# Regrouping q's columns by heads in a linear-attention block: token-major q tiles, a regrouped weight copy and six M passes

## The chip, the cores and the metric

The kernel runs on one core of a Trainium2 chip. The metric is the device time of one execution in microseconds (us). A core has TensorE (PE, with weight loads shown apart as PEld), VectorE (DVE), ScalarE (ACT), GpSimd (POOL) and SyncE (SP, which here only issues DMAs); each works through its own queue in order, and they meet through semaphores.

## The reference

The input x (2048 tokens of 640 features) is layernormed to xn, and three things are added:

```
qkv = xn @ wqkv                      # 32 heads of 20 features
pq, pk = phi(q), phi(k)              # phi(t) = t+1 if t > 0 else exp(t), + 1e-6
kv  = sum over tokens of pk (x) v    # 20 x 20 per head
z   = sum over tokens of pk
o   = (pq @ kv) / (pq . z + 1e-6)
A   = o @ wo
r   = xn @ w_r;  idx = the 8 tokens with the largest r
y   = (silu(xn[idx] @ w_gate) * (xn[idx] @ w_up)) @ w_down * sigmoid(r[idx])
out = x + A + xn + scatter_add(y at idx)
```

Everything is bf16 in memory, 640 = 5 x 128 features (five chunks), 2048 = 16 x 128 tokens (sixteen tiles).

## The kernel before, in words

The order on every engine is written out by hand: the program text is the order of each queue, nothing is rescheduled.

**Front.** The first x tiles and the weights wk and wq are loaded; VectorE takes batch statistics of each tile (two halves of 320, `ln_half`, L163), `ln_aggr` finishes mean and variance, and from tile 4 on GpSimd makes the scalars in four one-column instructions (L171, L176, L178, L179). `ln_norm` (L186) writes xn, and from tile 3 on issues a DMA transpose on SP's queue (L196) that makes xnT; tiles 0 to 2 are transposed on TensorE.

**Tile loop** (L401, t = 2 to 15; a "slot" below is one t). TensorE does k of tile t (`k_mm`, 10 matmuls: 5 chunks, 512 and 129 columns, token-major: tokens on the partitions), then `ga_mm` of tile t-1 (3 matmuls, part of G = xn^T pk), then q of tile t (`q_mm`, L244, 25 matmuls of 128 columns, feature-major: five blocks m of 128 features on the partitions, so that pqT needs no transpose). The weights of block m are the columns m, m+5, m+10 and so on of wq: a read with a step of 5. ScalarE takes exp and relu of each (`phi_act`); VectorE joins them (`phi_vec`, L225) into pk or pqT. VectorE's queue in a slot: statistics of tile t+3 (t+4 from slot 6 on; slot 5, `CATCH`, does two tiles), normalization of tile t+2 (slot 5 does two, later ones t+3), q_phi of t-1, k phi of t, from slot 12 also residual adds of x and xn. GpSimd makes small constants in slots 3 to 6 (`small_consts`). SP issues the later weight loads, one entry a slot (`late_loads`), behind the transposes; the residual is stored to a DRAM copy `xcp` (`keep`).

**Back half.** The column sums z of pk (`z_mm`), the remaining parts of G (`gb1`, then `gb2` into the PSUM pair gbC, five blocks a tile), eight candidates and their indices on VectorE; GpSimd gathers the 8 token columns into xsT (L537). The denominator `pden` is four column groups of 32 heads by 512 tokens; ScalarE makes its reciprocal as exp(-ln) (L580, L581), and it goes through DRAM (`rscr`) to come back as rows `rb` for all 128 partitions. `norm(j)` (L630) multiplies pqT by it, 512 tokens at a time. `gu` is the gate and up product of the 8 tokens, ScalarE's Sigmoid (which needs a table load, L584) and VectorE make hm, and TensorE transposes it (`ph`). `kv_mm` makes the per-head kv from wv and G, `kv_evict` masks it into kvT. `py` is the down product, stored with an accumulating indirect DMA into xcp (L697), and the residual is loaded back from there in six DMAs (L702).

**M** (L722) is kv @ wo, five chunks of 128 rows by 640 columns. With the step of 5 a group of 32 rows in a chunk belongs to 8 heads, that is to two blocks of 80 features; so each chunk takes two accumulating passes (i), each with four column groups (g) side by side on TensorE and 512 and 128 columns. PAD is the shift that puts the two blocks into the same 32 rows.

**Output** (L753): per tile five chunks by 512 and 128 columns into a PSUM pair (B, A, D, C in turn), VectorE adds the residual from PSUM (L751), and the tile is stored.

Of the kernel before, what the change touches and what calls it, by code (L numbers as in the profile page):

```python
# [8 lines left out]
P = 128  # L9
S = 2048  # L10
D = 640
H = 32
# [13 lines left out]
PAD = 16  # L26
# [3 lines left out]
WARM = 10  # L30
LAST = (0, 320, 512, 640)
CATCH = 5
# [12 lines left out]
def kernel(  # L45
# [42 lines left out]
    wq = sb([P, KC, D], BF16, "wq")  # L88
    wv = sb([P, KC, D], BF16, "wv")
# [3 lines left out]
    kvT = sb([EB, PAD + NEB * KC * 2 * PAD], BF16, "kvT")  # L93

    wd = sb([P, FC, D], BF16, "wd")
    xsT = sb([P, KC, 32], BF16, "xsT")
    hT = sb([P, FC, 32], BF16, "hT")
    rscr = dram.tile([NTB * P, TBLK], BF16, name="rscr")
# [32 lines left out]
    headg = sb([P, NTB, H], BF16, "headg")  # L131
    nc.vector.memset(headg[:], 1.0)
    mask80 = sb([EB, KC, 4, 4], BF16, "mask80")
# [20 lines left out]

    head_select(headg[:], [(0, NTB), (-4, H)], 1, 4)
# [87 lines left out]

    def q_mm(t, tag="B"):  # L244
        ps = pair(tag, f"q{t}")
        for m in range(KC):
            for kc in range(KC):
                nc.tensor.matmul(  # L248
                    ps[:, m * P : (m + 1) * P],
                    lhsT=wq[:, kc, m::KC],  # L250
                    rhs=xnT[:, kc, t * P : (t + 1) * P],
                    start=(kc == 0 and m in (0, 4)), stop=(kc == KC - 1),
                    skip_group_check=True,
                )
        return ps
# [47 lines left out]
    def small_consts(t):  # L303
        if t == 3:
# [5 lines left out]
        elif t == 4:  # L310
# [6 lines left out]
        elif t == 5:  # L317
# [23 lines left out]
    def late_loads(t):  # L341
        def part(dst, src, a, b):
# [4 lines left out]
            2: (x_sb, x_v, 8, 12), 5: (x_sb, x_v, 12, 16),  # L347
            6: (wg, kcF, 0, 2), 7: (wg, kcF, 2, 4), 8: (wg, kcF, 4, 5),
            9: (wu, kcU, 0, 2), 10: (wu, kcU, 2, 4), 11: (wu, kcU, 4, 5),
            12: (wv, wv_v, 0, 2), 13: (wv, wv_v, 2, KC), 14: (wo, wo_v, 0, 4), 15: (wo, wo_v, 4, 8),  # L350
            16: (wd, kcD, 0, 6), 17: (wd, kcD, 6, 12),
        }
        if t in plan:
            part(*plan[t])

# [12 lines left out]
    def q_phi(t, er):  # L368
        phi_vec(pqT[:, :, t * P : (t + 1) * P], er, True)
# [31 lines left out]
    for t in range(2, T):  # L401
# [196 lines left out]
    for t in range(2):  # L598
        gb2(t)
# [207 lines left out]
```

## Time and profile before

| what | value |
|---|---|
| median of 3 runs | 111.74 us (111.49 to 111.99) |
| the profiled execution | 111.62 us, span 109.9 us |
| granted TensorE clock | 1.00 |
| DVE, ACT, POOL busy, share of the span | 78%, 50%, 34% |
| instructions | 2999 |
| HBM read, written | 14.94 MB, 5.81 MB |

The span runs from the first to the last instruction of the execution; the difference to its time lies around it. Times within the trace are us from the start of the span. An entry of a timeline gives start, length, engine, line of the kernel, operation, output<-inputs and, in brackets, how long the engine stood idle before it and what ended that. An entry of the chain of waits gives start, length and what ran; there an instruction counts only until the next one takes over. A row of a group gives the count and then the busy us, the mean ns of one, and the idle time before them. Matmul ends are modelled, and busy TensorE time isn't time at its peak.

### The profile page before, as it was taken

What the parts mean: (1) busy time and instruction counts of PE and PEld (TensorE: products, weight loads), DVE (VectorE), ACT (ScalarE), POOL (GpSimd) and SP (SyncE); (2) the same over time, 40 slices, a digit from 0 to 9 for tenths busy, and PEclk for the clock granted to TensorE, in tenths of its full rate; (3) what the DMA queues carried; (4) which work ended last, traced back from release to release, by engine and by line L of the source; (5) the groups of instructions that cost most, each with busy time, mean ns of one, the idle gap of its engine ahead of it and who ended that gap; (6) DMA issues with size and microseconds to landing.
All of it is one profiled execution on the core that took longest, in us unless ns stands there. A gap on an engine that the chain in (4) does not pass through costs nothing.

```text
span 109.9 us, 2999 instructions
## 1 busy us (share of the span) xinstructions
PE 105.5 (96%) x1183; PEld 69.3 (63%) x1183; DVE 86.1 (78%) x205; ACT 55.1 (50%) x102; POOL 37.9 (34%) x83
## 2 busy tenths in 40 slices
PE   6998999999999999999999999999999999999990
PEld 2456866777577766777667744447995555555560
DVE  6889999887999889875999896951348967698680
ACT  4037987778867797777977745068028000000000
POOL 5414195989889955770000000240008100000000
DMA  2998164930569999998859970899541289997333
GB/s 72 335 375 292 33 36 75 283 66 3 118 177 321 220 267 280 316 305 224 290 187 285 292 257 5 232 378 372 175 145 51 15 228 323 340 387 277 128 119 119
DMA packets 25358, 23.09 MB, mean 210 GB/s; under 512 B 10624, under 2 KB 24064, under 8 KB 25344
## 3 DMA queue, kind: packets, MB, share of 16 engines
q1 hardware_dynamic: 22784, 20.43, 66.5%
q10 hardware_dynamic: 2384, 2.43, 6.4%
q8 instruction: 9, 0.15, 0.6%
q0 software_dynamic: 176, 0.04, 0.6%
q14 instruction: 5, 0.04, 0.1%
HBM read 14.94 MB, written 5.81 MB: 189 GB/s over the span
## 4 chain that ended last, share of the span: by engine, by line
PE 76%; DVE 10%; POOL 8%; issue 3%; DVEq 0%; POOLq 0%
PE o L743 14%; PE k L236 13%; PE q L248 13%; PE gbA L489 6%; PE gaC L259 5%; PE warm L271 4%; PE gbC L590 4%; POOL sq L176 3%; DVE st L163 2%; PE gaD L259 2%; DVE pk L225 2%; PE M L728 2%; POOL sc L178 2%; DVE xn L191 2%; PE gu L606 2%
## 5 line engine op out<-in xcount | busy, mean ns | idle before, releaser
L248 PEld LDWEIGHTS <-wq 128*128 128x128 bf16 x400 | 24.2, 117 | 3.4
L236 PE MATMUL k<-wk,xnT 128*128 128x512 bf16 (+1 forms) x160 | 24.8, 301 | 0.3 <-ACT xnT L206 0.3
L248 PE MATMUL q<-xnT,wq 128*128 128x128 bf16 x400 | 24.9, 220 | 0.0
L743 PEld LDWEIGHTS <-pqT 128*128 128x128 bf16 x165 | 12.8, 98 | 9.3
L236 PEld LDWEIGHTS <-xnT 128*128 128x128 bf16 x160 | 12.3, 98 | 8.5 <-ACT xnT L206 0.9
L213 ACT ACTIVATE eq<-q 128x640 bf16<-128x640 f32 x16 | 11.2, 703 | 10.5 <-PE q L248 10.5
L225 DVE SCALAR_TENSOR_TENSOR pk<-ek,rk 128x640 bf16<-128x640 bf16 x16 | 13.2, 824 | 3.6 <-ACT rk L216 3.4
L743 PE MATMUL o<-M,pqT 128*128 128x512 bf16 x110 | 15.8, 300 | 0.0
L176 POOL TENSOR_TENSOR sq<-sq,half 128x1 bf16<-128x1 bf16 x16 | 12.5, 778 | 6.2 <-DVE sc L175 4.0
L163 DVE BATCH_NORM_STATS2 st<-x_sb 128x6 f32<-128x320 bf16 x32 | 14.1, 480 | 0.4 <-DMA x_sb<-in_A_x_dram 0.4
L225 DVE SCALAR_TENSOR_TENSOR pqT<-eq,rq 128x640 bf16<-128x640 bf16 x16 | 13.2, 823 | 0.7 <-ACT rq L216 0.7
L213 ACT ACTIVATE ek<-k 128x640 bf16<-128x640 f32 x16 | 11.3, 705 | 1.6 <-PE k L236 0.4
L751 DVE TENSOR_TENSOR o_t<-o,x_sb 128x640 bf16<-128x640 f32 x11 | 8.8, 820 | 3.3 <-DMA x_sb<-xcp 1.7
L216 ACT ACTIVATE rq<-q 128x640 bf16<-128x640 f32 x16 | 11.2, 700 | 0.0
L216 ACT ACTIVATE rk<-k 128x640 bf16<-128x640 f32 x16 | 11.2, 699 | 0.0
L259 PE MATMUL gaC<-pk,xn 128*128 128x512 bf16 x32 | 9.5, 378 | 0.2 <-DVE pk L225 0.2
L537 POOL COPY xsT<-xnT 128x5 bf16 x8 | 1.9, 312 | 21.7 <-DVE icol L551 21.7
L178 POOL TENSOR_TENSOR sc<-sq,neg 128x1 f32<-128x1 bf16 x12 | 8.6, 716 | 0.9
L191 DVE TENSOR_SCALAR xn<-x_sb,sc 128x640 bf16<-128x640 bf16 (+2 forms) x17 | 6.9, 412 | 1.2 <-POOL sc L179 1.0
L489 PE MATMUL gbA<-pk,xn 128*128 128x512 bf16 x32 | 7.3, 380 | 0.0
L360 DVE TENSOR_TENSOR x_sb<-x_sb,xn 128x640 bf16<-128x640 bf16 x16 | 7.0, 482 | 0.0
L259 PEld LDWEIGHTS <-xn 128*128 128x128 bf16 x48 | 4.0, 97 | 4.1 <-issue 0.4
(152 smaller groups left out, 120.4 us busy)
## 6 DMA issues: line engine op xcount, KB each, us to landing
xcp<-x_sb SPq DMA_DIRECT2D x4, 640.0 KB, 5.2
x_sb<-in_A_x_dram SPq DMA_DIRECT2D x3, 640.0 KB, 4.7
wd<-in_B_w_down_dram SPq DMA_DIRECT2D x2, 960.0 KB, 6.6
x_sb<-xcp SPq DMA_DIRECT2D x3, 640.0 KB, 6.8
wg<-in_B_w_gate_dram SPq DMA_DIRECT2D x2, 768.0 KB, 6.6
wu<-in_B_w_up_dram SPq DMA_DIRECT2D x2, 768.0 KB, 5.3
out_dram<-o_t ACTq DMA_DIRECT2D x8, 160.0 KB, 2.7
out_dram<-o_t SPq DMA_DIRECT2D x7, 160.0 KB, 3.4
```

What stands on the lines that cost most here:

```text
L163: nc.vector.bn_stats(out=stat[t][:, h, :], in_=x_sb[:, t, h * HW : (h + 1) * HW])
L176: nc.gpsimd.tensor_tensor(out=sq[:, 1:2], in0=sq[:, 0:1], in1=half[:], op=ALU.pow)
L178: nc.gpsimd.tensor_tensor(out=sc[:, 1:2], in0=sq[:, 1:2], in1=neg1[:], op=ALU.pow)
L191: nc.vector.tensor_scalar(out=xn[:, t, a:b], in0=x_sb[:, t, a:b], scalar1=sc[:, 0:1], scalar2=sc[:, 1:2], op0=ALU.subtract, op1=ALU.mult,)
L213: nc.scalar.activation(e[:], ps[:, 0:D], AF.Exp)
L216: nc.scalar.activation(r[:], ps[:, 0:D], AF.Relu)
L225: nc.vector.scalar_tensor_tensor(out=dst, in0=ea, scalar=1.0, in1=ra, op0=ALU.min, op1=ALU.add)
L236: nc.tensor.matmul(ps[:, a:b], lhsT=xnT[:, kc, t * P : (t + 1) * P], rhs=wk[:, kc, a:b], start=(kc == 0), stop=(kc == KC - 1),)
L248: nc.tensor.matmul(ps[:, m * P : (m + 1) * P], lhsT=wq[:, kc, m::KC], rhs=xnT[:, kc, t * P : (t + 1) * P], start=(kc == 0 and m in (0, 4)) ...
L259: nc.tensor.matmul(gaC[:, c * TBLK : (c + 1) * TBLK] if c < 2 else gaD[:], lhsT=xn[:, t, c * P : (c + 1) * P], rhs=pk[:, t, 0:TBLK], start ...
L489: nc.tensor.matmul(gbA[:, (c - 3) * TBLK : (c - 2) * TBLK], lhsT=xn[:, t, c * P : (c + 1) * P], rhs=pk[:, t, 0:TBLK], start=(t == 0), stop ...
L743: nc.tensor.matmul(ps, lhsT=pqT[:, m, t * P : (t + 1) * P], rhs=M[:, m, a:b], start=(m == 0), stop=(m == KC - 1),)
```

## The change

Five things, together:

1. **q's columns by heads.** A feature's place is now: for each head the first 8 features, then the next 8, then the last 4. Chunks 0 to 3 hold 16 heads by 8 features each, chunk 4 all 32 heads by 4 features. Tiles 0 to 6 (`QTOK`) are computed token-major, with the xnT tile as weights and wq read through a regrouping view as the moving operand; phi goes to a buffer pqs, and seven DMA transposes on SP's queue in slots 5 to 9 bring it into pqT. Tiles 7 to 15 are feature-major as before, from wqp, a regrouped copy of wq that GpSimd makes in slots 2 to 5 (ten copies).
2. **Six M passes.** Chunks 0 to 3 take one pass each, chunk 4 two. kv_evict writes three pieces per half; z and the mask of heads (headm) follow the new order. py and its accumulating DMA stand between M chunks 0, 2 and 1, 3, 4.
3. **Reciprocal rows.** rden is stored once, and rb is three row sets (two of 16 heads by 8, one of 32 heads by 4), loaded in twelve DMAs; norm works on token ranges (0,2), (2,4), (4,8), (8,12), (12,16) with two instructions each. The copy of GT columns 3 and 4 moves behind rden.
4. **Order of the back half.** gb2 fills four blocks for 13 tiles, then ph, kv of the first four blocks, the last three tiles, then the fifth block for all tiles in another PSUM pair, then the rest of kv. The first four output tiles (`NPRE`) are copied out of PSUM by ScalarE and get their residual on VectorE from SBUF.
5. **Statistics and loads.** Half of tile 9's statistics are taken in slot 5, the other half in slot 6; the slot with two normalizations is slot 7 (tiles 9 and 10). The small constants move from slots 3 to 6 to slots 6 to 9, the weight loads come up to five slots earlier.

The diff, cut to what the text speaks of:

```diff
-CATCH = 5
+NPRE = 4
+QTOK = 7
+GB_A = 13
...
+    def regroup(ap):
+        v = ap.rearrange("p (h e) -> p h e", e=DH)
+        main = v[:, :, 0 : 2 * E8].rearrange("p h (c d) -> p c h d", c=2)
+        return (main, 0, TBLK), (v[:, :, 2 * E8 : DH], TBLK, D)
+
+    def wq_regroup(kc):
+        for src, a, b in regroup(wq[:, kc, :]):
+            shape = {"p (c h d) -> p c h d": dict(c=2, d=E8)} if a == 0 else {"p (h d) -> p h d": dict(d=E4)}
+            ((pat, kw),) = shape.items()
+            nc.gpsimd.tensor_copy(wqp[:, kc, a:b].rearrange(pat, **kw), src)
...
     def q_mm(t, tag="B"):
         ps = pair(tag, f"q{t}")
-        for m in range(KC):
-            for kc in range(KC):
+        if t >= QTOK:
+            for m in range(KC):
+                for kc in range(KC):
+                    nc.tensor.matmul(
+                        ps[:, m * P : (m + 1) * P],
+                        lhsT=wqp[:, kc, m * P : (m + 1) * P],
+                        rhs=xnT[:, kc, t * P : (t + 1) * P],
+                        start=(kc == 0 and m in (0, 4)), stop=(kc == KC - 1),
+                        skip_group_check=True,
+                    )
+            return ps
+        for kc in range(KC):
+            for rhs, a, b in regroup(wq[:, kc, :]):
                 nc.tensor.matmul(
-                    ps[:, m * P : (m + 1) * P],
-                    lhsT=wq[:, kc, m::KC],
-                    rhs=xnT[:, kc, t * P : (t + 1) * P],
-                    start=(kc == 0 and m in (0, 4)), stop=(kc == KC - 1),
-                    skip_group_check=True,
+                    ps[:, a:b],
+                    lhsT=xnT[:, kc, t * P : (t + 1) * P],
+                    rhs=rhs,
+                    start=(kc == 0), stop=(kc == KC - 1),
                 )
         return ps
...
-        for u in (t + 3, t + 4) if t == CATCH else (t + 3 + (t > CATCH),):
-            if u < T:
-                ln_stats(u)
-        for u in (t + 2, t + 3) if t == CATCH else (t + 2 + (t > CATCH),):
+        if t == 6:
+            ln_half(9, 1)
+            ln_aggr(9)
+        u = t + 3 + (t > 5)
+        if u < T:
+            ln_stats(u)
+        if t == 5:
+            ln_half(9, 0)
+        for u in (t + 2, t + 3) if t == 7 else (t + 2 + (t > 7),):
...
+        for kc in {2: (0,), 3: (1,), 4: (2,), 5: (3, 4)}.get(t, ()):
+            wq_regroup(kc)
...
+        for u in {5: (0,), 6: (1, 2), 7: (3,), 8: (4,), 9: (5, 6)}.get(t, ()):
+            nc.sync.dma_start_transpose(pqT[:, :, u * P : (u + 1) * P], pqs[:, u, :])
...
-    keep(T - 4, T)
-    nc.scalar.copy(GT[:, 3:5, 0:TBLK], two(gbA[:]))
...
     nc.scalar.activation(rden[:], lden[:], AF.Exp, scale=-1.0)
+    nc.scalar.copy(GT[:, 3:5, 0:TBLK], two(gbA[:]))
...
+    def rb_load(j):
+        lo = j * TBLK
+        for v in range(NV + 1):
+            h0, n, r = (v * HV, HV, E8) if v < NV else (0, H, E4)
+            (nc.scalar if (j, v) == (0, 1) else nc.sync).dma_start(
+                rb[:, v, lo : lo + TBLK],
+                rscr[32 * j + h0 : 32 * j + h0 + n, :].unsqueeze(1).to_broadcast([n, r, TBLK]),
+            )
+
+    nc.sync.dma_start(rscr[:], rden[:])
+    keep(T - 4, T)
+    for j in range(NTB):
+        rb_load(j)
...
+    kv_mm(0, range(4))
+    kv_evict(0)
+    for t in range(GB_A, T):
+        gb2(t, gbC, range(4))
+    nc.scalar.copy(GT[:, 0:4, TBLK:D], gbC[:, 0:TBLK].rearrange("p (c f) -> p c f", c=4))
+    gbB = pair("B", "gbB")
+    for t in range(T):
+        gb2(t, gbB, (4,))
+    nc.scalar.copy(GT[:, 4, TBLK:D], gbB[:, 0:P])
+    norm(0, 2)
+    kv_mm(1, (0, 1))
+    kv_mm(1, (2, 3), range(4))
+    kv_mm(1, (2, 3), (4,))
+    kv_evict(1)
...
+    def m_row(m, tag, copy):
+        pm = Acc(tag, f"M{m}")
+        for x in (None,) if m < 4 else (0, 1):
+            for a, b in halves:
                 for g in range(4):
-                    o = PAD + ((2 * g + i) * KC + m) * 2 * PAD - i * PAD
+                    if m < 4:
+                        blk = 4 * (m % 2) + g
+                        k0 = 64 * blk + 32 * (m // 2)
+                    else:
+                        blk = 2 * g + x
+                        k0 = 512 + 32 * blk - 16 * x
...
+    m_row(0, "C", nc.scalar.copy)
+    m_row(2, "B", nc.scalar.copy)
+    py = pair("A", "py")
...
+    m_row(1, "D", nc.vector.tensor_copy)
+    m_row(3, "A", nc.scalar.copy)
+    m_row(4, "C", nc.vector.tensor_copy)
+    norm(2, 4)
+    norm(4, 8)
...
+    for t in range(NPRE):
+        po = Acc("BDAC"[t % 4], f"o{t}")
+        for m in M_ORDER:
+            for a, b in halves:
+                out_mm(t, po.at(a, b), m, a, b)
+        o_pre[t] = o_tile(t)
+        for a, b in po.spans:
+            nc.scalar.copy(o_pre[t][:, a:b], po.at(a, b))
+    for t in range(NPRE):
+        nc.vector.tensor_tensor(out=o_pre[t][:], in0=o_pre[t][:], in1=x_sb[:, t, :], op=ALU.add)
+        (nc.scalar, nc.sync)[t % 2].dma_start(out_v[:, t, :], o_pre[t][:])
+    norm(8, 12)
+
+    for t in range(NPRE, T):
+        if t == 8:
+            norm(12, 16)
```

More of the change, by code (lines that the diff above doesn't have):

```diff
@@ L647, with kv_mm @@
     )
-    for t in range(12, T):
-        gb2(t)
-    nc.scalar.copy(GT[:, :, TBLK:D], gbC[:, 0:D].rearrange("p (c f) -> p c f", c=KC))
-    pkv = (bank("D0", "pkv0"), bank("D1", "pkv1"), pair("B", "pkv2"))
-    groups = ((0, 2, 4), (1, 3, 5), (6, 7))
-    def kv_mm(i):
-        for n, b in enumerate(groups[i]):
-            for kc in range(KC):
+    pkv = bank("D0", "pkv0"), bank("D1", "pkv1")
+    def kv_mm(i, ns, kcs=range(KC)):
+        for n in ns:
+            b = 4 * i + n
+            for kc in kcs:
                 nc.tensor.matmul(
```

212 lines of the change are left out of this document (107 added, 105 removed).

## Prediction

> **What bounds the kernel now.** I read the page first: which engine is busy, and how long.
>
> ```profile
> PE 105.5 (96%) x1183; PEld 69.3 (63%) x1183; DVE 86.1 (78%) x205; ACT 55.1 (50%) x102; POOL 37.9 (34%) x83
> ```
>
> TensorE (PE) is busy for 96% of the span, so PE time taken out comes off the end, and every new PE wait is paid in full. The profiled execution took 111.62 us around a span of 109.9; the median of the three timed runs is 111.74, so I work against 111.62 and take the 0.12 as noise. About 0.5% (0.56 us) is what a measurement of this kernel can tell from no change.
>
> Second, the PE timeline of the tile loop (start, length, instruction, wait before it), and the same stretch in the chain that ended last.
>
> ```profile
> 27.66 1.55 PE L236 MATMUL k<-wk,xnT 128*128 128x512 bf16 x10
> 29.44 0.59 PE L259 MATMUL gaC<-pk,xn 128*128 128x512 bf16 x2 [0.23 <-DVE pk L225]
> ```
>
> ```profile
> 30.25 1.40 PE q L248 x25
> 31.64 1.38 PE k L236 x10
> ...
> 35.07 1.38 PE k L236 x10
> ```
>
> The k pass takes 1.38, so the ga pass that began at 29.44 was due at 29.05: a hole of 0.39 in slot 6, because pk(5) came late from VectorE (DVE). It is the only hole that the change can remove in the loop; otherwise a slot of the loop is 3.43 us (31.64 to 35.07) of unbroken PE work.
>
> Third, what made pk late. The chain in front of that ga pass, and POOL's timeline and groups:
>
> ```profile
> 27.47 0.45 DVE xn L191
> 27.92 0.73 DVE pqT L225
> 28.65 0.75 DVE pk L225
> ```
>
> This is VectorE's order in a slot: a normalization, q's phi, k's phi. It had stood waiting for GpSimd (POOL), which finishes the layernorm scalars of each tile in four one-column instructions:
>
> ```profile
> 17.36 0.41 POOL L179 CAST sc<-mv 128x1 f32<-128x1 bf16 x1
> 18.86 0.30 POOL L171 TENSOR_SCALAR sq<-mv 128x1 bf16<-128x1 bf16 x1 [1.09 <-DVE mv L167]
> ```
>
> ```profile
> L176 POOL TENSOR_TENSOR sq<-sq,half 128x1 bf16<-128x1 bf16 x16 | 12.5, 778 | 6.2 <-DVE sc L175 4.0 <-DVE sq L171 1.1
> L178 POOL TENSOR_TENSOR sc<-sq,neg 128x1 f32<-128x1 bf16 x12 | 8.6, 716 | 0.9
> ...
> L171 POOL TENSOR_SCALAR sq<-mv 128x1 bf16<-128x1 bf16 x12 | 3.8, 317 | 6.8 <-DVE mv L167 6.8
> L179 POOL CAST sc<-mv 128x1 f32<-128x1 bf16 x12 | 3.6, 298 | 0.0
> ```
>
> The means add to 2.11 us a tile, about 2.2 with the handovers. POOL is 34% busy over the span, but in slots 3 to 7 it has little to spare: the average hides a stage in which it is nearly the bound.
>
> **The tile loop, part by part.** *q on PE.* A token-major tile needs 10 matmuls in place of 25, over the same 3,200 columns. The k pass has that shape and takes 1.38 against q's 1.40: 7 x 0.02 = 0.1 us. The other nine tiles keep 25 matmuls of 128 columns, already at 56 ns each; contiguous weights can't speed a stream that isn't waiting for them. Gain 0.1.
>
> *The hole.* Slot 5 loses half of a tile's statistics and one normalization on DVE, so pk(5) is in time: gain 0.39. VectorE has room for the half moved to slot 6.
>
> *The regrouped copy on POOL.* Ten copies are added in slots 2 to 5, two for each of five weight chunks: 512 and 128 elements a partition. They stand in POOL's queue behind that slot's statistics and ahead of the next one's. No row shows such a copy. The nearest:
>
> ```profile
> L150 POOL TENSOR_SCALAR_AFFINE_SELECT mask<-mask 80x80 bf16<-80x80 bf16 x1 | 0.6, 624 | 0.1
> L146 POOL TENSOR_SCALAR_AFFINE_SELECT mask<-mask 80x80 bf16<-80x80 bf16 x1 | 0.4, 431 | 0.0
> masks.py:199 POOL TENSOR_SCALAR_AFFINE_SELECT ident<-ident 128x128 bf16<-128x128 bf16 x1 | 0.3, 291 | 0.1
> L311 POOL TENSOR_SCALAR_AFFINE_SELECT selm<-selm 4x4 f32<-4x4 f32 x1 | 0.2, 183 | 0.0
> ```
>
> 124 more elements cost 108 ns, 0.87 ns each. So a 512-element copy alone is 0.183 + 508 x 0.87 ns = 0.63, a 128-element one 0.29, and a chunk, R, is 1.02 with handovers. That is the lower end. The mask operations have 80 elements, worth 0.25, but ran inside the loop beside DVE and took 0.43 and 0.62. With both extras (0.18 + 0.37) on a chunk, R is 1.57, the upper end. I take 1.35, a little nearer to the rows of the loop, since all ten copies run there.
>
> What that does: tile 5's scalars end at 17.77. From there POOL has five chunks and the scalars of tiles 6 to 10 to do, in that order, with no gap to lose: it ends tile 10 at 17.77 + 5R + 5L. At R = 1.35 and L = 2.1 (a little under 2.2, as DVE will partly stand still and leave POOL alone) this is 35.0. Slot 7 has two normalizations, tiles 9 and 10, and in VectorE's queue q_phi(6) and pk(7) stand behind them: 0.45 + 0.73 + 0.75 = 1.93, 1.95 with the handover, after tile 10's scalars: 36.97. ga(7) is due at 27.66 + 2 x 3.43 + 1.38 = 35.90. **PE waits 1.05 us in slot 8.** The wait is zero up to R = 1.14 and grows by 0.5 for each 0.1 beyond; at 1.57 it is 2.15. The deferred constants now follow tile 10's scalars and may delay tile 11's a little; not counted.
>
> The GPSIMD Engine Reference of the Trainium skill, section 4.1 (Engine selection), speaks against that wait: it calls one-input elementwise work on GpSimd roughly line-rate. By the page R would be near the lower end, and the sum 1.05 less; the 0.87 ns slope agrees with it, the mask rows inside the loop don't.
>
> *SP's queue.* Each DMA transpose holds SP for 1.2 us, and seven are added, ahead of weight loads that come three slots earlier than before:
>
> ```profile
> 30.76 1.21 SPq L196 DMA_TRANSPOSE xnT<-xn  x1
> 32.03 0.57 SPq L343 DMA_DIRECT2D wg<-in_B_w_gate_dram  x1
> ```
>
> ```profile
> xnT<-xn SPq DMA_TRANSPOSE x13, 3.9
> ```
>
> In slot 6 SP gets three transposes and two loads (estimate 3.6 + 1.1 = 4.7 us in a 3.43 us slot), so, with tile 8's transpose going out about 2 us into the slot, at 29.7, tile 9's goes out near 34.4 and lands 3.9 later, at 38.3. k(9) is due at 27.66 + 3 x 3.43 = 37.95 and with the 1.05 wait is due at 39.0: hidden by that wait, and worth 0.35 where it is absent. Later transposes have three slots of lead.
>
> **The back half, part by part.** The chain from the denominator to the first output tile:
>
> ```profile
> 72.03 1.19 PE pden L571 x20
> ...
> 73.89 1.74 PE gu L606 x40
> 75.62 2.90 PE gbC L590 x50
> ...
> 81.34 0.94 PE py L688 x48
> 82.28 1.63 PE M L728 x48
> ...
> 85.00 2.82 PE o L743 x20
> ```
>
> *M.* It runs from 82.28 to 85.00: ten passes (five chunks, two blocks each) of 0.272. Six passes are 1.63: **gain 1.09**. Counts of gb2, pkv, py and z are unchanged; their order costs nothing in itself.
>
> *The wait at ph.* The copy of GT columns 3 and 4 moves from before the denominator to between rden and the Sigmoid table load on ScalarE:
>
> ```profile
> 72.06 1.01 ACT L565 CAST GT<-gbA 128x1024 bf16<-128x1024 f32 x1 [4.32 <-PE gbA L489]
> 73.27 0.69 ACT L580 ACTIVATE lden<-pden,eps 128x512 f32<-128x512 f32 x1 [0.20 <-PE pden L571]
> ...
> 74.64 1.28 ACT L584 ACT_TABLE_LOAD   x1
> ```
>
> ```profile
> 77.14 0.56 DVE L617 TENSOR_TENSOR hm<-gu,hm 128x384 bf16<-128x384 f32 x1
> ```
>
> Before, the copy lay beside pden and lden waited for PE, not for it. Now table load, Sigmoid and hm all come 0.95 to 1.01 later: hm ends near 78.66, not 77.70. PE meanwhile has gu at 73.22 to 74.96 and 52 gb2 matmuls at 58 ns, 3.02: it stands at ph at 77.98. **Wait 0.68.** Bounds: 0.5 to 0.8.
>
> *M3* goes into the PSUM pair that py leaves, and y's copy stands behind M2's on ScalarE: wait 0.1. Output starts at 85.00 - 1.09 + 0.68 + 0.1 = 84.69.
>
> *The return of y.* py now ends two M passes of 0.27, M4's two and that 0.1 ahead of the output: 84.69 - 1.18 = 83.51, against 82.28. Rows of the reload and of what hangs on it:
>
> ```profile
> 87.19 2.90 SPq L702 DMA_DIRECT2D x_sb<-xcp  x6
> ```
>
> ```profile
> 91.87 0.69 DVE L751 TENSOR_TENSOR o_t<-o2a,x_sb 128x512 bf16<-128x512 f32 x1 [0.77 <-DMA x_sb<-xcp]
> ...
> 94.34 0.82 DVE L751 TENSOR_TENSOR o_t<-o,x_sb 128x640 bf16<-128x640 f32 x1 [0.86 <-DMA x_sb<-xcp]
> ```
>
> ```profile
> L632 DVE TENSOR_TENSOR pqT<-pqT,rb 128x2560 bf16<-128x2560 bf16 x4 | 5.9, 1485 | 0.7 <-DMA rb<-rscr 0.7
> L360 DVE TENSOR_TENSOR x_sb<-x_sb,xn 128x640 bf16<-128x640 bf16 x16 | 7.0, 482 | 0.0
> ```
>
> With y 1.3 later (1.23 and its copy's queue), x tiles 2 and 3 land at 93.2. The first four output tiles no longer hold PSUM for that: ScalarE copies them. But on VectorE stand, in order, the adds of tiles 2 and 3 (2 x 0.41 start to start), norm(8, 12) (about 1.6: the 1.485 row plus a second instruction) and the add of tile 4 (0.82): 93.2 + 0.8 + 1.6 + 0.8 = 96.4. Tile 8 wants tile 4's PSUM at 84.69 + 8 x 1.38 to 1.41, 95.7 to 96.0. **Wait 0.6**, bounds 0 and 0.9; tile 4's own residual at 94.34 + 1.3 gives the same. After it VectorE gains on PE, and the last tile ends as now.
>
> At nothing I cost: the smaller row store and twelve row loads, since norm(0, 2) and kv_evict(1) are due only near 82 (cover gone, each us late is a us late for M1); the memsets at the start, beside the first load; evictions in three pieces, beside M0, M2 and py.
>
> **Sum.** 111.62 - 0.39 - 0.1 + 1.05 - 1.09 + 0.68 + 0.1 + 0.6 = 112.47. Predicted 112.5; this case alone reaches from 111.8 to 113.6 (wait in the loop 0.4 to 2.15).
>
> **Rivals.** *POOL in time, the other side.* Place: POOL's queue in slots 2 to 6; it decides at R = 1.14. Then no wait in slot 8, 0.35 at k(9) at most, and 111.4 to 111.8. For it: the slope, and 1.09 us of POOL idle at 18.86 that the first chunk fills. Against: the mask rows. *POOL in time and the reload too:* as before, without the 0.6 at tile 8, the 0.35 at k(9), and with ph at its lower bound: 111.62 - 1.58 + 0.6 = 110.6. For it: the bounds above reach there; against: two chains must both be kinder than their rows. *The strided stream.* The token-major tiles and z read their moving operand in runs of 8 elements. The rows of the present strided weight reads against contiguous ones:
>
> ```profile
> L248 PEld LDWEIGHTS <-wq 128*128 128x128 bf16 x400 | 24.2, 117 | 3.4
> ...
> L743 PEld LDWEIGHTS <-pqT 128*128 128x128 bf16 x165 | 12.8, 98 | 9.3
> ```
>
> If a moving stream lost the same 19%, seven passes of 1.38 would cost 1.84 more: 114.3. Against: runs of 8, not single elements. SBUF — State Buffer of the Trainium skill, section Door 1, says that a read which crosses to a new 16-byte line pays, and that two hits a line keep the full rate; no row here shows which holds for these runs. *SP late.* Tile 9's transpose behind a fuller DMA queue, 1.5 late beyond the POOL wait: about 113.5.
>
> **How the numbers follow.** Forecast 0.45; POOL in time 0.25; POOL and reload in time 0.17; strided stream 0.07; SP late 0.06. The range takes the forecast's own and most of the two quicker cases, and leaves the strided one out: 110.5 to 114.0. Faster by over 0.5% (under 111.2): 0.17 and 0.09 of the second case, 0.26. Within: the rest of the second and the low end of the first, 0.16 + 0.07 = 0.23. Slower: 0.51.
>
> **What would show it.** POOL's regroup rows (R), the end of tile 10's scalars (35.0), PE's wait before ga in slot 8 named for pk; no hole in slot 6; the wait before ph named for hm, 0.7; M in 1.6 us of PE; a wait at output tile 8 named for o_t's adds; q passes of 1.38 in the seven tiles. Wrong if the copies take under 1.0 a chunk, if q's passes lengthen, or if ScalarE's table load still begins near 74.6.

## The result, and the profile after

The changed kernel takes 115.23 us (median of four runs, 114.62 to 116.43); beside it on the same chip the kernel before took 111.78 (111.49 to 111.99). The ratio is 1.0293, 95% interval 1.0235 to 1.035: slower by about 3%. The forecast of 112.5 had the sign and missed the size; 115.23 lies above its range.

The profiled execution is the longest of the four (116.43 us, span 114.7) and a slow one; the ratios here and below leave out such executions, and the other three have a median of 114.95. Some 1.6 us of it is a lower granted clock in us 41 to 45, which the other three don't have (clock 1.00 over the span).

TensorE's waits by releaser, the kernel after (us in total, times, longest):

```profile
PE k L244 <- DMA xnT<-xn: 2.0, 1, 2.0
...
PE ph L697 <- DVE hm L666: 0.8, 1, 0.8
...
PE o L818 <- DVE M L784: 0.3, 1, 0.3
...
PE M L776 <- ACT y_sb L800: 0.2, 1, 0.2
```

Two are in the forecast: ph (0.68 there, 0.80 here) and M3's wait for y's copy (0.1 there, 0.21 here). Two are not: k(9) waits for the transposed tile 9, and the first output tile for M's last chunk. The forecast's two largest new waits, in slot 8 for pk(7) and at output tile 8, are missing. The rows left out between these belong to the front of the kernel, where executions differ: slot 2 begins at 14.32 here, at 13.71 to 14.06 in the other runs of the change, and at 13.95 before. The TensorE timeline of the same kernel has the places:

```profile
28.11 1.54 PE L244 MATMUL k<-wk,xnT 128*128 128x512 bf16 x9
29.50 0.59 PE L288 MATMUL gaC<-pk,xn 128*128 128x512 bf16 x2
...
31.56 0.65 PE L244 MATMUL k<-wk,xnT 128*128 128x512 bf16 x3
...
40.57 2.08 PE L244 MATMUL k<-wk,xnT 128*128 128x512 bf16 x10 [1.96 <-DMA xnT<-xn]
...
45.66 1.55 PE L244 MATMUL k<-wk,xnT 128*128 128x512 bf16 x9
...
82.67 0.34 PE L697 MATMUL ph<-ident,hm 128*128 128x128 bf16 x3 [0.80 <-DVE hm L666]
...
88.08 1.00 PE L776 MATMUL M<-wo,kvT 80*32 80x512 bf16 x24 [0.21 <-ACT y_sb L800]
89.24 1.03 PE L818 MATMUL o<-M,pqT 128*128 128x128 bf16 x7 [0.16 <-issue]
90.61 0.43 PE L818 MATMUL o<-M,pqT 128*128 128x512 bf16 x2 [0.34 <-DVE M L784]
```

Slot 6 runs from 28.11 to 31.56 without its hole. k(9) was due at 28.11 + 3 x 3.45 = 38.46 and began at 40.57. The chain of waits names why (start, length, what ran):

```profile
34.05 0.45 DVE xn L199
34.49 0.73 DVE pqs L233
35.23 0.74 DVE pk L233
35.96 0.46 DVE st L171 x2
36.42 4.10 DMA xnT<-xn
```

The chain goes through VectorE only because it follows events. On VectorE's timeline tile 9 was normalized at 32.81 to 33.21 (0.40, L199), 3.2 us before its transpose went out. What was in between is on SP's timeline:

```profile
30.38 1.21 SPq L204 DMA_TRANSPOSE xnT<-xn  x1
31.63 2.62 SPq L387 DMA_TRANSPOSE pqT<-pqs  x2
34.29 0.58 SPq L378 DMA_DIRECT2D wg<-in_B_w_gate_dram  x1
34.91 1.41 SPq L378 DMA_DIRECT2D wv<-in_A_wqkv_dram  x1
36.42 2.53 SPq L204 DMA_TRANSPOSE xnT<-xn  x2
```

This is slot 6 in SP's queue: tile 8's transpose, two of the new ones, two weight loads, 6.0 us in a slot of 3.45, and only then tile 9's. It landed at 40.52, after 4.10 us, near the median of 3.9: what was late was its start.

GpSimd's timeline shows that the step forecast as the bound was none:

```profile
18.07 0.85 POOL L261 COPY wqp<-wq 128x512 bf16<-128x512 bf16 x2
...
22.00 1.01 POOL L261 COPY wqp<-wq 128x512 bf16<-128x512 bf16 x2
...
28.39 1.64 POOL L261 COPY wqp<-wq 128x512 bf16<-128x512 bf16 x4
```

A chunk costs 0.8 to 1.0 us, not 1.35. Tile 10's scalars end at 34.01 (forecast 35.0), and TensorE has no wait in slot 8.

What the lower clock behind k(9)'s wait did is in the windows of the same execution (stretch and its length; busy us of PE, PEld, DVE, ACT and POOL, with the number of instructions; granted clock; share of the DMA engines; GB/s):

```profile
41.00:42.00 1.00, 1.00 (x8) 0.53 (x6) 1.00 (x2) 0.00 (x0) 0.92 (x2) 0.71 0.53 78
42.00:43.00 1.00, 1.00 (x6) 0.45 (x4) 0.00 (x1) 0.32 (x1) 0.84 (x4) 0.50 0.66 123
```

At this clock k's pass takes 2.08 instead of 1.54, and slot 9 takes 5.09 us (40.57 to 45.66) instead of 3.45.

Stretch by stretch on TensorE, from start to start and against the kernel before, the profiled execution loses 0.37 us ahead of slot 2 (the front, which varies), 2.16 from k(7) to k(9), 1.66 in slot 9, 0.20 in the rest of the way to pden, 0.29 from pden to the first output matmul and 0.49 from there to the end; it gains 0.37 in slot 6. That is the 4.8 us between the spans of 114.7 and 109.9.

### The profile page after: what moved, and what is told of

The parts are those of the page before. It is cut to its first block, busy times and chain, and to the rows that moved or that the text cites. A ratio compares the mean times of both kernels' runs of the same rounds, so it can differ in the third digit from the quotient of the medians.

```text
span 114.7 us, 2777 instructions
## 1 busy us (share of the span) xinstructions
PE 104.8 (91%) x1034; PEld 64.7 (56%) x1046; DVE 85.3 (74%) x219; ACT 58.5 (51%) x107; POOL 41.5 (36%) x101
## 2 busy tenths in 40 slices
DMA packets 30861, 24.87 MB, mean 217 GB/s; under 512 B 15488, under 2 KB 29568, under 8 KB 30848
## 4 chain that ended last, share of the span: by engine, by line
PE 54%; POOL 14%; DVE 11%; DMA 10%; ACT 3%; issue 3%; SPq 1%; ACTq 0%; DVEq 0%; POOLq 0%
PE o L818 12%; PE k L244 10%; PE q L268 9%; PE gbA L542 6%; DMA wk<-in_A_wqkv_dram 5%; POOL sq L184 4%; DMA xnT<-xn 4%; POOL sc L186 4%; PE gaC L288 3%; POOL wqp L261 3%; DVE st L171 3%; POOL sq L179 2%; DVE pk L233 2%; PE gaD L288 2%; PE M L776 2%
## 5 line engine op out<-in xcount | busy, mean ns | idle before, releaser
L244 PEld LDWEIGHTS <-xnT 128*128 128x128 bf16 x160 | 12.5, 98 | 12.1 <-DMA xnT<-xn 2.1
L818 PE MATMUL o<-M,pqT 128*128 128x128 bf16 (+1 forms) x108 | 15.7, 297 | 0.5 <-DVE M L784 0.3
L268 PEld LDWEIGHTS <-wqp 128*128 128x128 bf16 x225 | 13.9, 101 | 2.4 <-issue 0.6
L268 PE MATMUL q<-xnT,wqp 128*128 128x128 bf16 x225 | 14.6, 223 | 0.0
L184 POOL TENSOR_TENSOR sq<-sq,half 128x1 bf16<-128x1 bf16 x16 | 11.4, 710 | 7.2 <-DVE sc L183 4.5
L278 PE MATMUL q<-wq,xnT 128*128 128x512 bf16 x70 | 11.0, 303 | 0.0
L233 DVE SCALAR_TENSOR_TENSOR pqT<-eq,rq 128x640 bf16<-128x640 bf16 x9 | 7.4, 822 | 1.7 <-ACT rq L224 1.7
L199 DVE TENSOR_SCALAR xn<-x_sb,sc 128x640 bf16<-128x640 bf16 (+2 forms) x17 | 7.0, 417 | 2.1 <-POOL sc L187 1.9
L278 PEld LDWEIGHTS <-xnT 128*128 128x128 bf16 x70 | 5.6, 96 | 5.2
L186 POOL TENSOR_TENSOR sc<-sq,neg 128x1 f32<-128x1 bf16 x12 | 7.9, 656 | 0.9
L590 POOL COPY xsT<-xnT 128x5 bf16 x8 | 1.2, 219 | 19.3 <-DMA zrel<-zpart 19.3
L826 DVE TENSOR_TENSOR o_t<-o,x_sb 128x640 bf16<-128x640 f32 x8 | 6.4, 819 | 1.5 <-PE o L818 1.0
```

The source lines that it names most:

```text
L184: nc.gpsimd.tensor_tensor(out=sq[:, 1:2], in0=sq[:, 0:1], in1=half[:], op=ALU.pow)
L186: nc.gpsimd.tensor_tensor(out=sc[:, 1:2], in0=sq[:, 1:2], in1=neg1[:], op=ALU.pow)
L233: nc.vector.scalar_tensor_tensor(out=dst, in0=ea, scalar=1.0, in1=ra, op0=ALU.min, op1=ALU.add)
L244: nc.tensor.matmul(ps[:, a:b], lhsT=xnT[:, kc, t * P : (t + 1) * P], rhs=wk[:, kc, a:b], start=(kc == 0), stop=(kc == KC - 1),)
L268: nc.tensor.matmul(ps[:, m * P : (m + 1) * P], lhsT=wqp[:, kc, m * P : (m + 1) * P], rhs=xnT[:, kc, t * P : (t + 1) * P], start=(kc == 0 a ...
L278: nc.tensor.matmul(ps[:, a:b], lhsT=xnT[:, kc, t * P : (t + 1) * P], rhs=rhs, start=(kc == 0), stop=(kc == KC - 1),)
```

## The experiments

All of them change the kernel after, but for the eighth, which changes the kernel before. Medians, ratios to the kernel before as it ran beside them on the same chip, and 95% intervals:

| kernel | us | ratio |
|---|---|---|
| after | 115.23 | 1.0293 (1.0235 to 1.035) |
| e1_tr_late | 120.91 | 1.0805 (1.0719 to 1.0891) |
| e2_loads_late | 115.65 | 1.0345 (1.0251 to 1.0438) |
| e3_no_copy | 115.98 | 1.0359 (1.0282 to 1.0436) |
| e4_gt_early | 115.34 | 1.0277 (1.0186 to 1.0368) |
| e5_no_tr | 112.18 | 1.0036 (1.0001 to 1.0071) |
| e6_q4 | 113.45 | 1.0145 (1.0107 to 1.0182) |
| e7_q4_back | 113.28 | 1.0155 (1.0091 to 1.0218) |
| e8_before_stats | 111.66 | 0.9991 (0.9963 to 1.0018) |
| e9_py_early | 112.13 | 1.005 (1.001 to 1.009) |
| e10_no_tr_back | 111.35 | 0.9983 (0.9954 to 1.0013) |
| e11_q3_best | 112.77 | 1.0126 (1.0054 to 1.0198) |
| e12_sp_only | 118.79 | 1.0637 (1.0597 to 1.0677) |

The kernel before took 111.61 us beside e1 to e4, 111.88 beside e5 to e8, 111.76 beside e9 to e11 and 111.77 beside e12.

### Is it GpSimd's copies?

```diff
-        for kc in {2: (0,), 3: (1,), 4: (2,), 5: (3, 4)}.get(t, ()):
-            wq_regroup(kc)
...
-                        lhsT=wqp[:, kc, m * P : (m + 1) * P],
+                        lhsT=wq[:, kc, m * P : (m + 1) * P],
```

> The changed kernel without the ten regrouping copies on GpSimd; tiles 7 to 15 read blocks of wq as they lie, so q's features of these tiles stand in another order and the output isn't the reference's, with the same instructions on all other engines. Theory A: xn(9) is not what is late, its transpose waits in SP's queue, so k(9) still waits about 2; 114.3 to 115.3 us. Theory B, and the prediction's own step (copies of 1.35 us a chunk; the trace shows 0.79 to 0.95): the wait goes, 112.5 to 113.2 us.

115.98 us. Without any copy k(9) waits as before, longer even, in the TensorE timeline:

```profile
41.16 2.85 PE L244 MATMUL k<-wk,xnT 128*128 128x512 bf16 x10 [2.57 <-DMA xnT<-xn]
```

Tile 9's transpose goes out at 35.23 here and takes 5.88 us to land. The copies are not the cause.

### Is it the transposes and loads in SP's slots 5 to 9?

First the transposes moved out of the way, and the load of wd, which shares pqs's place, behind them:

```diff
-        for u in {5: (0,), 6: (1, 2), 7: (3,), 8: (4,), 9: (5, 6)}.get(t, ()):
+        for u in {11: (0, 1), 12: (2, 3), 13: (4, 5), 14: (6,)}.get(t, ()):
...
-        elif t in (10, 11):
-            part(late["wd"], kcD, 6 * (t - 10), 6 * (t - 9))
+        elif t in (14, 15):
+            part(late["wd"], kcD, 6 * (t - 14), 6 * (t - 13))
```

> The changed kernel with the seven DMA transposes of pqs moved from slots 5 to 9 to slots 11 to 14 (two a slot), and the wd load that follows them to slots 14 and 15. Theory A (SP's queue: in the changed kernel xn(9) was ready at 33.2 but its transpose was issued only at 36.42, behind two pqs transposes and two loads, and k(9) waited until 40.57 instead of 38.45): xnT(9) is issued by 34.5, the wait at k(9) goes, and with it the stretch at a granted clock of 0.5 where there was one; 112.3 to 113.0 us. Theory B (GpSimd's regrouped copies make xn(9) and xn(10) late): nothing changes in that queue, 114.6 to 115.5 us.

120.91 us, slower still; no theory gave that. TensorE's two waits say why:

```profile
38.42 1.56 PE L244 MATMUL k<-wk,xnT 128*128 128x512 bf16 x10 [0.39 <-DMA xnT<-xn]
...
79.79 0.72 PE L622 MATMUL pden<-pqT,zm 128*32 128x512 bf16 x4 [7.60 <-DVE zm L596]
```

k(9) is down to 0.39, so the transposes ahead of it were its cause. (Its own transpose now goes out in time, at 32.69; the 0.39 is a landing time of 5.68 us.) But the queue's debt moved: zm needs the column sums zrel, which are tiny transfers behind everything else in the same queue. In SP's timeline of e1:

```profile
59.83 2.44 SPq L387 DMA_TRANSPOSE pqT<-pqs  x1
66.83 0.39 SPq L378 DMA_DIRECT2D wd<-in_B_w_down_dram  x1
...
70.49 2.37 SPq L532 DMA_DIRECT2D zrel<-zpart  x2
```

wd shares pqs's place and can't be written until the last transposes have landed, so the queue stands from 62.3 to 66.8 (SP's waits name pqT<-pqs, 4.4 us in two). z begins at 63.58 in e1; in e5 below, where it begins at 63.12, zrel goes out at 65.84 and here at 70.49, and in the chain of waits its last part takes 7.10 to land.

Then the two loads of slot 6 moved to slots 10 and 11 instead:

```diff
-            6: (wg, kcF, 4, 5), 7: (wu, kcU, 0, 2), 8: (wu, kcU, 2, 4), 9: (wu, kcU, 4, 5),
+            10: (wg, kcF, 4, 5), 7: (wu, kcU, 0, 2), 8: (wu, kcU, 2, 4), 9: (wu, kcU, 4, 5),
...
-        if t == 6:
+        if t == 11:
             part(wv, wv_v, 0, 2)
```

> The changed kernel with only the two weight loads of slot 6 (wg's last part, wv's first) moved to slots 10 and 11; the transposes stay. They held SP from 34.29 to 36.32 and stood in front of tile 9's transpose. Theory A: the transpose is issued about 2.0 earlier, the wait of 2.1 at k(9) shrinks to 0 to 0.5; 112.5 to 113.5 us. If the two pqs transposes in front are the greater part, the wait stays over 1 us and the time over 113.8. Theory B: 114.6 to 115.5 us.

115.65 us: no quicker, though the wait at k(9) shrinks to 0.81. Others come in later slots, in TensorE's timeline:

```profile
39.37 1.56 PE L244 MATMUL k<-wk,xnT 128*128 128x512 bf16 x10 [0.81 <-DMA xnT<-xn]
53.77 1.56 PE L244 MATMUL k<-wk,xnT 128*128 128x512 bf16 x10 [0.53 <-DMA xnT<-xn]
58.02 1.56 PE L244 MATMUL k<-wk,xnT 128*128 128x512 bf16 x9 [0.65 <-DMA xnT<-xn]
62.31 1.56 PE L244 MATMUL k<-wk,xnT 128*128 128x512 bf16 x10 [0.69 <-DMA xnT<-xn]
```

So the order of loads and transposes decides who waits. The next run takes the transposes out and leaves the rest in place:

```diff
-        phi_vec(pqs[:, t, :], er, False)
+        phi_vec(pqT[:, :, t * P : (t + 1) * P], er, True)
...
-            nc.sync.dma_start_transpose(pqT[:, :, u * P : (u + 1) * P], pqs[:, u, :])
```

> The changed kernel without its seven transposes of q: phi of tiles 0 to 6 is written token-major straight into the place of pqT, so these tiles' rows of the output are left out. Everything else, the earlier weight loads too, is as in the changed kernel. Theory A (the seven transposes on SP's queue are what delays xnT, and so k): no wait of k for xnT over 0.4 us from slot 9 on, and the loop's 2 to 4 us of such waits go: 112.0 us (111.4 to 112.8). Theory B (the weight loads that come earlier keep the DMA engines busy, whatever the transposes do): k(9) still waits over 1 us and the time stays above 114.

112.18 us, as the first theory had it: no k waits for xnT any more, and the seven transposes cost about 2.9 us (the ratios 1.0293 and 1.0036, times 111.8). What remains of the change is then 0.3 to 0.4 us slower than the kernel before.

Last, SP's time without the transposes' packets:

```diff
-            nc.sync.dma_start_transpose(pqT[:, :, u * P : (u + 1) * P], pqs[:, u, :])
+            for i in range(4):
+                nc.sync.dma_start(
+                    scr[64 * u + 16 * i : 64 * u + 16 * i + 16, :],
+                    pqT[16 * i : 16 * i + 16, i, u * P : u * P + 32],
+                )
```

> The changed kernel with each of the seven transposes replaced by four small stores on the same queue in the same place (16 partitions by 32 elements each, to a scratch in DRAM): they hold SP for about as long as a transpose (4 times some 0.35 us against 1.27) but give the DMA engines 64 packets in place of 672. Phi of tiles 0 to 6 is written token-major into pqT's place, so these tiles' rows of the output are left out. Theory A (SP's queue: three transposes and two loads in one slot make tile 9's own transpose late): xnT(9) still goes out after 35.5 us, k(9) waits over 1 us, and the time is 114 us or more. Theory B (the DMA engines: the transposes' packets delay everything that lands between slots 6 and 15, and SP's own time does not matter): no wait of k over 0.4, 112.2 us (111.7 to 112.9).

118.79 us: SP's queue makes the wait without the transposes' load on the DMA engines. SP's timeline and TensorE's:

```profile
31.48 5.08 SPq L388 DMA_DIRECT2D scr<-pqT  x8
...
37.60 2.54 SPq L204 DMA_TRANSPOSE xnT<-xn  x2
```

```profile
41.94 2.85 PE L244 MATMUL k<-wk,xnT 128*128 128x512 bf16 x10 [3.00 <-DMA xnT<-xn]
```

The dose was too large: four small stores held SP 2.54 us in this slot and 1.96 in others, not the 1.27 of a transpose, so the size of the wait can't be compared, but its place can. Tile 9's transpose goes out 1.2 us later than in the kernel after and takes 4.30 to land, and k(9) waits 1.0 longer (k(8) waits 0.47), with a fifth of the packets: the page counts 27053, e5's 26157, that is 128 for a tile's four stores (not 64, as the expectation had it), where a transpose has 672 (30861 less 26157, by seven). Beyond slot 9 this run has no wait of k, so for the later waits SP's time alone is not shown to be the cause. The chain of waits of e4 (its edit, below, lies behind the loop) shows a second part, at k(14):

```profile
52.52 7.11 DMA xnT<-xn
```

Tile 14 was normalized at 48.80, stood 3.7 us behind SP's queue, and then took 7.11 us to land, against a median of 4.3 in that run. By these figures, as an estimate, k(14), due at 58.41, would have been served with either part alone. Why some transposes land so late is not shown; the longest is 5.7 us in the kernel before, 7.9 in the kernel after, 8.3 in e4 and 6.4 in e5.

### Fewer transposes

Four token-major tiles instead of seven, with three chunks copied ahead of the loop, one transpose a slot, and the loads of wv and wd later:

```diff
-QTOK = 7
+QTOK = 4
...
     qp = q_mm(0, "A")
+    for kc in range(3):
+        wq_regroup(kc)
...
-        for kc in {2: (0,), 3: (1,), 4: (2,), 5: (3, 4)}.get(t, ()):
-            wq_regroup(kc)
+        if t in (2, 3):
+            wq_regroup(t + 1)
...
-        for u in {5: (0,), 6: (1, 2), 7: (3,), 8: (4,), 9: (5, 6)}.get(t, ()):
+        for u in {6: (0,), 7: (1,), 8: (2,), 9: (3,)}.get(t, ()):
```

> Four token-major tiles instead of seven: three of the five chunks of the regrouped copy are made on GpSimd ahead of the loop, where its rows show 2.5 us without work, the others in slots 2 and 3; four transposes, one each in slots 6 to 9; wv's loads in slots 10 and 11, wd's in 11 and 13. No slot then has more than one transpose of q and one or two loads on SP. Theory A (it is the overfull slots of SP's queue, three transposes and two loads in 3.45 us): the waits of k go but for at most 0.5 in all: 112.2 us (111.6 to 113). Rival (each further transpose costs by itself, on the DMA engines): four sevenths of the cost stay, 113.5 to 114.

113.45 us, at the edge of the rival's range. TensorE waits 0.44 before k(8) and 0.43 before pden, where zm comes late. The first isn't SP's queue: tile 8's transpose goes out at 30.09, right behind its normalization, and takes 5.35 us to land. So a transpose that doesn't overfill a slot doesn't seem free either, but with the loads moved too this run alone doesn't show its price. Part of pden's wait is no transpose: zpart is now copied in the new order, 1.31 us on ScalarE instead of 0.69, and stands in the chain ahead of zrel; e5 has the same copy and no wait.

### The other steps

The hole in slot 6 by itself, in the kernel before:

```diff
+        if t == 6:
+            ln_half(9, 1)
+            ln_aggr(9)
+        u = t + 3 + (t > 5)
...
+        if t == 5:
+            ln_half(9, 0)
+        for u in (t + 2, t + 3) if t == 7 else (t + 2 + (t > 7),):
```

> The kernel before with one part of the change alone: tile 9's statistics half in slot 5 and half in slot 6, the two normalizations in slot 7, the small constants on GpSimd in slots 6 to 9. The prediction's step gives 0.39 from the hole in slot 6: 111.2 us (0.997 of before). Rival: the hole only moves to a later slot, and the time stays at that of before, 111.6.

111.66 us, ratio 0.9991: the rival. The hole goes, and three slots on as much is paid again (0.41 idle, 0.57 from start to start):

```profile
27.45 1.55 PE L236 MATMUL k<-wk,xnT 128*128 128x512 bf16 x10
30.88 1.55 PE L236 MATMUL k<-wk,xnT 128*128 128x512 bf16 x9
34.30 1.55 PE L236 MATMUL k<-wk,xnT 128*128 128x512 bf16 x10
38.30 0.94 PE L236 MATMUL k<-wk,xnT 128*128 128x512 bf16 x4 [0.41 <-DMA xnT<-xn]
```

This kernel has no added transposes and no earlier loads. With the normalization of tile 9 moved from slot 6 to slot 7, its transpose goes out at 32.56 instead of 30.76 and takes 5.69 us to land: this part of the change by itself uses up the slack of k(9).

The copy of GT back ahead of the denominator:

```diff
+    nc.scalar.copy(GT[:, 3:5, 0:TBLK], two(gbA[:]))
     pden = bank("D0", "pden")
...
     nc.scalar.activation(rden[:], lden[:], AF.Exp, scale=-1.0)
-    nc.scalar.copy(GT[:, 3:5, 0:TBLK], two(gbA[:]))
```

> The changed kernel with the copy of GT columns 3 and 4 back ahead of the denominator, as before the change. The trace of the changed kernel shows PE waiting 0.80 at ph. Theory of that step: Sigmoid and hm come 0.95 earlier, the wait at ph goes, and 0.7 to 0.8 us with it: 114.1 to 114.4 us against 114.9 to 115.1 of the changed kernel. Rival: hm's 0.8 is given back at the next wait (rows of the reciprocal, y's return): under 0.3 us.

115.34 us. The wait at ph is gone, and the time doesn't show it: k's waits in the loop add to 3.9 us in this execution (1.98 in slot 9, 0.67 in slot 13, 1.27 in slot 14). Against so much that varies, 0.8 can't be read from the time. The loop is that of the kernel after, at a granted clock of 1.00: it loses 2.19 us from k(7) to k(9), nothing in slot 9, and 2.35 between k(10) and pden, where the profiled execution of the kernel after lost 0.12. So the later waits belong to the changed loop; that the stretch at the lower clock hid them there, by giving the queue time, is likely and not shown.

With four token-major tiles k's waits are small (0.44 in e6), and the back half can be read. e7 has that edit and M's chunk 4 ahead of chunk 3:

```diff
-    m_row(3, "A", nc.scalar.copy)
     m_row(4, "C", nc.vector.tensor_copy)
+    m_row(3, "A", nc.scalar.copy)
...
-    M_ORDER = (0, 2, 1, 3, 4)
+    M_ORDER = (0, 2, 1, 4, 3)
```

> The one with four token-major tiles, and two edits behind the loop: the copy of GT columns 3 and 4 back ahead of the denominator, and M's chunk 4 ahead of chunk 3 (also in the output's sum), so that chunk 4 and not chunk 3 stands behind the copy of y. Theory A: the waits at ph (0.8), before M3 (0.2) and at output tile 0 (0.3) go, and the end follows: 1.0 to 1.3 under the same kernel without them, near 111.1. Rival (the return of y or the adds set the end of the output stage, as the forecast had it at tile 8): the gain is eaten there, under 0.5 left.

113.28 us against e6's 113.45: the rival again. ph and M3 wait no longer, but the first output tile waits 0.45 for chunk 3's copy, now the last, and TensorE stands 1.23 at output tile 8:

```profile
84.61 1.13 PE L820 MATMUL o<-M,pqT 128*128 128x128 bf16 x7 [0.16 <-issue]
86.18 0.43 PE L820 MATMUL o<-M,pqT 128*128 128x512 bf16 x2 [0.45 <-ACT M L786]
...
97.35 1.52 PE L820 MATMUL o<-M,pqT 128*128 128x512 bf16 x10 [1.23 <-DVE o_t L828]
```

VectorE's timeline shows the chain that the prediction wrote down, from the reload of tiles 2 and 3 over a normalization to the add of tile 4:

```profile
93.85 0.89 DVE L843 TENSOR_TENSOR o_t<-o_t,x_sb 128x640 bf16<-128x640 bf16 x2 [2.19 <-DMA x_sb<-xcp]
94.66 1.22 DVE L690 TENSOR_TENSOR pqT<-pqT,rb 128x2048 bf16<-128x2048 bf16 x1
95.80 0.42 DVE L693 TENSOR_TENSOR pqT<-pqT,rb 128x512 bf16<-128x512 bf16 x1
96.47 0.82 DVE L828 TENSOR_TENSOR o_t<-o,x_sb 128x640 bf16<-128x640 f32 x1 [0.26 <-DMA x_sb<-xcp]
```

e9 tests that chain by its start. py, y's store and the reload move up, the block itself unchanged:

```diff
     nc.scalar.copy(GT[:, 0:4, TBLK:D], gbC[:, 0:TBLK].rearrange("p (c f) -> p c f", c=4))
+    py = pair("A", "py")
...
     gbB = pair("B", "gbB")
```

> The kernel with four token-major tiles, the early copy of GT columns 3 and 4 and M's chunk 4 ahead of chunk 3, which stood 1.2 us at output tile 8 behind VectorE's adds; now the down product py, the copy of y, its store and the reload of the residual also stand earlier, right behind the 13 plus 3 tiles of gb2. Theory A (tile 8 waits because y comes back late, as the prediction's chain has it): y goes out about 2 us earlier, the wait of 1.2 goes, 112.1 us (111.7 to 112.6). Rival (the reload is slow because the DMA engines are full at that time, whenever it starts): the wait at tile 8 keeps at least half, 112.7 or more.

112.13 us, 1.15 less than e7, as forecast: the wait at tile 8 is gone. This is the fastest version with the whole computation and six M passes, and it is still 0.1 to 0.9% slower than the kernel before.

The same back half (the edits of e7 and e9) without the transposes:

```diff
-        phi_vec(pqs[:, t, :], er, False)
+        phi_vec(pqT[:, :, t * P : (t + 1) * P], er, True)
...
+    nc.scalar.copy(GT[:, 3:5, 0:TBLK], two(gbA[:]))
     pden = bank("D0", "pden")
...
+    py = pair("A", "py")
...
     gbB = pair("B", "gbB")
...
-    M_ORDER = (0, 2, 1, 3, 4)
+    M_ORDER = (0, 2, 1, 4, 3)
```

> What the rest of the change is worth when the waits that it brought are gone: without the seven transposes (phi of tiles 0 to 6 written token-major into pqT's place, so these tiles' rows of the output are left out), with the early copy of GT columns 3 and 4, M's chunk 4 ahead of chunk 3, and py early. Theory A (the six M passes give their 1.1 and the hole 0.4 once nothing is put in their place): 112.2 less 0.8 (ph), 0.2 (M3) and 0 to 0.3 (first output tile): 111.0 us (110.4 to 111.4). Rival (something else that the change added, not seen as a wait of TensorE, holds the end): 111.6 or more.

111.35 us; 0.9983 (0.9954 to 1.0013), the same as the kernel before within the measurement, and at the upper end of the first theory's range. The waits view lists none for TensorE's matmuls from slot 2 on, and yet the middle of that range, 111.0, isn't reached. It is 0.78 under e9, the price of four transposes if the other differences of the two cost nothing. The M passes show where some of the gain goes:

```profile
81.89 0.73 PE L793 MATMUL M<-wo,kvT 80*32 80x512 bf16 x16
82.63 0.40 PE L793 MATMUL M1a<-wo,kvT 80*32 80x512 bf16 x4
82.96 0.24 PE L793 MATMUL M1b<-wo,kvT 80*32 80x128 bf16 x4
83.14 1.00 PE L793 MATMUL M<-wo,kvT 80*32 80x512 bf16 x24
84.07 1.53 PE L815 MATMUL o<-M,pqT 128*128 128x512 bf16 x9
```

Six passes of 0.272 are 1.63; from 81.89 to 84.07 it takes 2.18. Chunk 1 waits for VectorE's second eviction of kv, which py covered in the kernel after: the rows of M's weight loads stand idle 0.34 and 0.23 us, both named for kvT. The ten passes before took 2.72 with no gap. So the net gain of M is 0.54, half of what was counted; in the kernel after M and py together take 3.20 (86.04 to 89.24) against 3.66 before (81.27 to 84.93), which is 0.46.

Last, an attempt to beat both: three token-major tiles (transposes in slots 7, 9 and 10), wd behind zrel as before, and the first two output tiles interleaved, on top of e9's back half:

```diff
-QTOK = 7
+QTOK = 3
...
-        for u in {5: (0,), 6: (1, 2), 7: (3,), 8: (4,), 9: (5, 6)}.get(t, ()):
+        for u in {7: (0,), 9: (1,), 10: (2,)}.get(t, ()):
...
+    late_loads(T)
+    late_loads(T + 1)
     nc.scalar.copy(GT[:, 0:2, 0:TBLK], two(gaC[:]))
...
+    pre2 = [Acc("BD"[t], f"o{t}") for t in range(2)]
+    for ms in (M_ORDER[:4], M_ORDER[4:]):
+        for t in range(2):
+            for m in ms:
+                for a, b in halves:
+                    out_mm(t, pre2[t].at(a, b), m, a, b)
```

> An attempt at a kernel quicker than both, complete in what it computes: three token-major tiles with one transpose each in slots 7, 9 and 10, three chunks of the regrouped copy ahead of the loop and two in slot 2, wv's loads in slots 10 and 11, wd's behind the column sums as in the kernel before; behind the loop the early copy of GT columns 3 and 4, py early, M's chunk 4 ahead of chunk 3, and the first two output tiles do their first four chunks each before the last chunk. Theory A (waits of k under 0.5 in all, of pden for zm none, of ph, M3 and the first output tile none): 110.9 us (110.3 to 111.6). Rival (each transpose keeps costing its share of the DMA engines, three sevenths of 3 us): 112 or more.

112.77 us: a miss, the rival's number, and not quicker than e9. Its profiled execution, the fastest of four at 111.79, has 0.37 before a k and 0.2 before a q that waits for the copies; what makes the others longer is not shown. No version tried here beats the kernel before.

## Why the prediction was wrong, step by step

- **The step that failed** is SP's queue: "tile 9's goes out near 34.4 and lands 3.9 later, at 38.3. k(9) is due at 27.66 + 3 x 3.43 = 37.95 and with the 1.05 wait is due at 39.0: hidden by that wait". It went out at 36.42 and landed at 40.52. The sum of the slot was short: 4.7 us forecast, 6.0 measured (the wv load held SP 1.41, not about 0.5), and it began at 30.38, not 29.7. Tile 9's transpose then took 4.10 to land, about as forecast. The wv load stands there because it came forward six slots, from 12 to 6, not three or up to five as the text says of the loads. The step also leaned on another wait as its cover, and that wait did not exist. e1, e5 and e12 show this cause.
- "**Later transposes have three slots of lead**" was wrong as well: e2 and e4 have waits of 0.5 to 1.3 as late as 62 us. The lead of a tile is what its queue and its landing time leave of it (3.7 us late and 7.1 to land for tile 14 in e4). Together the transposes cost about 2.9 us (e5), for which the sum had nothing. The rival "SP late" had the mechanism, with 1.5 us and a chance of 0.06; its 113.5 should by its own terms be 114.0.
- **The sign** was right by luck. The forecast was slower because of the 1.05 in slot 8 and the 0.6 at output tile 8, and neither wait came; without them its sum is 110.8, quicker than the kernel before.
- **The regrouped copy** was mis-sized: R = 0.8 to 1.0 in place of 1.35, under the threshold of 1.14 which the text gave itself. The extras taken from the mask operations inside the loop did not apply. The GPSIMD Engine Reference of the Trainium skill, section 4.1, spoke for the lower value; the trace agrees with it.
- **The hole** is worth 0.39 where it stands, and nothing alone: e8 pays 0.41 at k(9). The text had a price at this place ("worth 0.35 where it is absent"), but laid it to the fuller queue; that the later normalization of tile 9 takes the slack by itself it didn't count.
- **Token-major q** gains nothing: a q pass of slot 2 runs from 16.35 to 17.77, 1.42, beside 1.40 before. Nor did the strided stream cost 19%: SBUF — State Buffer of the Trainium skill, section Door 1, has two hits a line at full rate, and the trace agrees for these runs of 8 elements.
- **ph** was right: 0.80 against 0.68, and e4 removes it by undoing the move named.
- **M** was right in its count and half right in its worth, 0.54 net (e10), 0.46 in the kernel after. With ph's 0.80 that is why the stretch from pden to the output lost 0.29 instead of gaining. Not foreseen: the first output tile waits 0.34 for chunk 4's copy. **M3's wait** of 0.1 was 0.21.
- **Tile 8** didn't wait in the kernel after, where the output stage began later than forecast (13.26 us from pden's start to the first output matmul, 75.98 to 89.24, against 12.66 in the working); that this gave the reload its time is argued. The chain itself was right: e7 makes the output earlier and waits 1.23, and e9 removes that by its start.
- One thing stays open: from the start of the last three adds to the end of the span it takes 3.87 us after (110.83 to 114.7) and 3.45 before (106.45 to 109.9). SP's own waits place it: the last wait for output stores to land is 1.2 us after and 0.6 before. Why they land later is not shown.

## What to carry to other kernels

Add up, for each slot, what an issuing queue has to issue, in its order, before calling a transfer hidden: a queue that is over its slot makes late whatever stands behind it, and moving the surplus can just choose another victim, perhaps the one tiny transfer that everything waits for. Then add the landing time, by its longest and not its median. Do not hide one estimate behind another estimated wait. When a wait is taken away from a chain with several near-critical partners, ask for each partner how much slack it had; here 0.4 at k(9) ate the hole's gain (e8), and 1.2 at output tile 8 ate what e7 removed.

## What the runs showed of the hardware

- After TensorE stood for 1.96 us (kernel after), 2.57 (e3) or 3.0 (e12), the granted clock fell to about 0.5 for 3 to 6 us in the profiled execution. After 1.98 us in e4 it did not: the row of granted clocks on e4's page is 9 throughout, the one on e12's page (tenths, 40 slices) has the dip:

```profile
PEclk9999999999999955899999999999999999999998
```

The price of a dip isn't seen in the times: e12 took 118.61 us in an execution with a clock of 1.00 over the span and 118.71 with 0.967.

- A store of 1 KB (16 partitions by 32 elements) holds SP for 0.49 to 0.64 us (1.96 for four, 5.08 for eight), no less than most weight loads of hundreds of KB (0.42 to 0.58), so splitting transfers is paid for at the queue.
- The DMA transpose of a tile (128 by 640) holds SP for 1.21 to 1.30 us in most places, and up to 4.22 behind wd's loads in e4; it lands 2.7 to 8.3 us after it goes out.
- On GpSimd a pair of strided copies of 512 and 128 bf16 elements takes 0.8 to 1.0 us, beside a busy VectorE.
